# Reciprocals of the attention denominators: from a VectorE reciprocal to a GpSimd power of minus one

## The chip, the cores and the metric

The kernel runs on one core of a Trainium2 chip. The metric is the device time of one execution in microseconds (us). The kernel before has a median of 163.22 us over three runs (163.11, 163.22, 165.66). The engines are written as in the profile: PE (TensorE matmuls), PEld (its weight loads), DVE (VectorE), ACT (ScalarE), POOL (GpSimd), SP (SyncE, whose queue issues all the DMAs here).

## The reference, cut to what matters

Two independent results are put side by side along the last axis: A, a long convolution by FFT over 2048 positions and 576 channels, and B, a block of linear attention with 32 heads of 18 channels. The change touches B alone:

```python
qkv = (x @ wqkv).reshape(B, S, 3, H, Dh)...        # S 2048, D 576, H 32, Dh 18
phi = lambda t: jnp.where(t > 0, t + 1, jnp.exp(t)) + 1e-6
pq, pk = phi(q), phi(k)
kv = jnp.einsum("bhsd,bhse->bhde", pk, v)
z = jnp.einsum("bhsd->bhd", pk)
num = jnp.einsum("bhqd,bhde->bhqe", pq, kv)
den = jnp.einsum("bhqd,bhd->bhq", pq, z)[..., None] + 1e-6
o = num / den
return o... @ wo
```

The division is the place of the change: one denominator for each of 2048 positions and 32 heads, 65536 numbers.

## The kernel before, in words

The kernel is written as a list of operations that are recorded with their reads and writes (`P.op`). The order in which they are issued is fixed by hand-kept text: PLAN (L850 to L887) names the operations one after the other, each with the engine's letter (P, A, D, G for POOL, S for SP) and its number, and PLACES gives each buffer its address. Every engine has its own queue and works it strictly in that order; an instruction that waits holds up all that stand behind it on the same engine. Parts A and B are woven together so that PE has work nearly all the time.

Part A first forms a short convolution of k with four taps and multiplies it with v (`conv_piece`, L384). There are six pieces, three column groups by two halves. Each is two products on DVE (L395, 128x3072), a sum of 3072 and a sum of 1536 (L399 and L402) and a product with v (L404); the sums and the product go through the helper `tt` (L234) on DVE or POOL, as PLAN says. PE then transforms v (`s1`, L456), ACT or DVE copy the result out of PSUM as Cu (L227 and L229 in `copy`), DVE transposes it (L495), PE transforms again (L504), products with the filter's transform follow, and PE transforms back (L540, L565).

Part B projects x to pk (L604, L609, L612) and to pqT (L625, L628, L631), forms G from x and pk (L654), from G the masked matrices kvb (L692) and zsel (L707, L710), and from kvb and wo the matrix M (L751). The denominators follow from pqT and zsel:

- PE forms them in two halves f of 1024 positions (L729). A half lies as 128 partitions x 256 elements: 4 groups of 256 positions by 32 rows for the heads.
- DVE adds a column (L736), which gives `den`, 128x256 float32.
- DVE takes the reciprocal (L742), which gives `rden`, 128x256 bfloat16.
- SP writes `rden` to a scratch in memory (`rw`, twice for each half) and reads it back with each head's row repeated 9 times (`rr`, into `rb`), all L220.
- DVE or POOL multiply pqT by rb (`pqn`, L766, through L234). One of the five pieces of half 0 is on DVE, the other four and all five of half 1 on POOL.
- PE multiplies the normalised pqT by M (L794); the first of these matmuls needs all five pieces of half 0.

The order around the change, from PLAN (L868 to L870):

```
A202 A203 A220 G80 D240 S671 D243 A218
D81 S672 S244 D88 D87 S245 P204 D89 A540 A205 P610 S630 S258 A611 P606 S252 P604 A605 P214 D253 A607 S257 S250 P616
D90 S246 A617 A215 D91 P612 G251 P618
```

D240 and D243 are the two reciprocals. G80 is the sum of 1536 of a convolution piece on POOL, and D81 the product with v that reads G80's result; P610 is the first transform that reads D81's. D88 and D87 are the next piece's two tap products (L395), D89, D90 its sums and D91 its product with v. S244 and S245 write half 0, S258 and S257 half 1, and S252 reads back the piece that D253 multiplies (`pqn` on DVE); S258 stands ahead of S252 on SP. G251 is the first `pqn` on POOL.

Operations marked `two` (the sums and products of two SBUF tensors) have one more rule: when one of them is on POOL, it waits for the last marked operation that DVE has in the order ahead of it (L842 to L847). The reciprocals are not marked.

Of the kernel before, what the change touches and what calls it, by code (L numbers as in the profile page):

```python
# [11 lines left out]
ALU = mybir.AluOpType  # L12

S = 2048
D = 576
EPS = 1e-6
# [97 lines left out]
def _tables():  # L114
    import ml_dtypes
    bf = ml_dtypes.bfloat16
    w0 = 2.0 * np.pi / 8192.0
    k2 = np.arange(128)
    a = np.arange(128)
    b = np.arange(16)  # L120
    n = 16 * a[:, None] + b[None, :]
    ph = ((4 * k2[None, None, :] - 1) * n[:, :, None]) % 8192
    G = np.empty((128, 16, 2, 128), np.float32)
    G[:, :, 0, :] = np.cos(w0 * ph)
    G[:, :, 1, :] = -np.sin(w0 * ph)
    E = np.empty((128, 32 + 2, 128), np.float32)
    phe = ((4 * k2[:, None, None] - 1) * n.T[None, :, :]) % 8192
    E[:, 0:32:2, :] = np.cos(w0 * phe) / 2048.0
    E[:, 1:32:2, :] = -np.sin(w0 * phe) / 2048.0
    W = np.zeros((32, 3, 32), np.float32)  # L130
    for bb in range(16):
        for k1 in range(16):
            p = 2.0 * np.pi * ((k1 * bb) % 16) / 16.0
            c, s = np.cos(p), np.sin(p)
            W[bb, 0, 2 * k1] = c
            W[16 + bb, 0, 2 * k1] = s
            W[bb, 0, 2 * k1 + 1] = -s
            W[16 + bb, 0, 2 * k1 + 1] = c
            W[2 * k1, 1, 2 * bb] = c
            W[2 * k1 + 1, 1, 2 * bb] = -c  # L140
            W[2 * k1, 1, 2 * bb + 1] = s
            W[2 * k1 + 1, 1, 2 * bb + 1] = -s
            W[2 * k1, 2, 2 * bb] = -s
            W[2 * k1 + 1, 2, 2 * bb] = -s
            W[2 * k1, 2, 2 * bb + 1] = c
            W[2 * k1 + 1, 2, 2 * bb + 1] = c
    W[np.abs(W) < 1e-7] = 0.0
    for i in range(2):
        E[:, 32 + i, :] = np.kron(np.eye(4), W[:, 1 + i, :])

    C1 = np.zeros((128, 128 + 32 + 128), np.float32)
    C1[:, 0:128] = np.eye(128)
    C1[:, 128:160] = np.tile(W[:, 0, :], (4, 1))
    C1[:, 160:288] = np.kron(np.eye(4), W[:, 0, :])
    C = np.zeros((128, 32 + 640 + 126 + 8), np.float32)
    o = 0
    hm = np.zeros((128, 5, 128), np.float32)
    for c, (h0, hn) in enumerate(HCH):
        for m in range(hn):
            hm[m, c, 96 + 7 * c + m // 18] = 1.0  # L160
    C[0, o:o + 32] = 1.0
    o += 32
    C[:, o:o + 640] = hm.reshape(128, 640)
    o += 640
    m = np.arange(126)
    C[:126, o:o + 126] = (m[:, None] // 18 == m[None, :] // 18)
    o += 126
    C[:, o:o + 8] = EPS
    return G.astype(bf), E.astype(bf), C1.astype(bf), C.astype(bf)


# [11 lines left out]
def kernel(  # L183
# [13 lines left out]
    nc = tc.nc  # L197
    x, wqkv, wo = B_x[0], B_wqkv, B_wo
    q, k, v = A_q[0], A_k[0], A_v[0]
    outd = out[0]  # L200
    Gt, Et, C1t, Ct = _tables()
    Gp = np.zeros((2, 128, 2304), Gt.dtype)
    Gp[:, :, 0:2048] = Gt.reshape(128, 2, 2048).transpose(1, 0, 2)
# [6 lines left out]
    P = Prog()  # L210
# [25 lines left out]
    def psb(banks, name):  # L236
        return P.buf(name, [128, banks, 512], FP32, space="ps", banks=banks)
# [4 lines left out]
    cst = SB("cst", [128, Ct.shape[1]], side=1)  # L242
# [18 lines left out]
    def cs(o, n):  # L261
        return cst.t[:, o:o + n]
# [28 lines left out]
    for hh in range(2):  # L291
        wps = psb(4, "wps")

        def wmm(e, hh=hh, wps=wps):
# [5 lines left out]
            out=Wj.t[:, :, HALF * hh:HALF * hh + HALF], in_=wps.t[:, :, 0:HALF], func=ACTF.Copy),  # L300
            rd=[wps], wr=[(Wj, hh)], name="Wj", n=1152)
# [367 lines left out]
    for t in range(5):  # L669
# [8 lines left out]
         wr=[(wo5, "m")])  # L678
# [7 lines left out]
    def kvmm(e):  # L686
# [6 lines left out]
        out=kvb.t[0:126, 0:4, :], in0=kps.t[0:126, 0, 0:504].rearrange("p (c m) -> p c m", c=4),  # L693
        in1=maskbd()[0:126, :].unsqueeze(1).to_broadcast([126, 4, 126]), op=ALU.mult),
        rd=[kps, cst], wr=[(kvb, 0)], name="kvev", n=504)
    P.op("D", lambda e: nc.vector.tensor_tensor(
        out=kvb.t[0:72, 4, 0:72], in0=kps.t[0:72, 1, 0:72], in1=maskbd()[0:72, 0:72], op=ALU.mult),
        rd=[kps, cst], wr=[(kvb, 1)], name="kvev", n=72)
    zps = psb(1, "zps")

    def zmm(e):
# [6 lines left out]
        out=zsel.t[0:126, 0:4, :], in0=zps.t[0:126, 0, 0:128].rearrange("p (c m) -> p c m", c=4),  # L708
        in1=hmask()[0:126, 0:4, 96:128], op=ALU.mult), rd=[zps, cst], wr=[(zsel, 0)], name="zev", n=128)
    P.op("D", lambda e: nc.vector.tensor_tensor(  # L710
        out=zsel.t[0:72, 4, :], in0=zps.t[0:72, 0, 128:160], in1=hmask()[0:72, 4, 96:128], op=ALU.mult),
        rd=[zps, cst], wr=[(zsel, 1)], name="zev", n=32)
    dcol = SB("dcol", [128, 1], FP32)
    rdens = []
    for f in range(2):
        dps = psb(2 - f, "dps")
        den = SB("den", [128, 256], FP32)
        rden = SB("rden", [128, 256])
        rdens.append(rden)

        def dmm(e, f=f, dps=dps):
            if f == 0:
                for c, (h0, hn) in enumerate(HCH):
                    for g in range(4):
                        nc.tensor.matmul(dps.t[32 * g:32 * g + 32, 1, 0:1], lhsT=zsel.t[0:hn, c, :], rhs=epsc()[0:hn, :],
                                         start=(c == 0), stop=(c == 4))
            for c, (h0, hn) in enumerate(HCH):
                for g in range(4):
                    nc.tensor.matmul(dps.t[32 * g:32 * g + 32, 0, 0:256], lhsT=zsel.t[0:hn, c, :],  # L729
                                     rhs=pqT[f].t[0:hn, c, 256 * g:256 * g + 256], start=(c == 0), stop=(c == 4))  # L730
        P.op("P", dmm, rd=[zsel] + [(pqT[f], (c, g)) for c in range(5) for g in (2 * f, 2 * f + 1)] + ([cst] if f == 0 else []), wr=[dps],
             name="den", mm=[(256, 128, 128)] * 6)
        if f == 0:
            P.op("D", lambda e, dps=dps: nc.vector.tensor_scalar_add(out=dcol.t[:], in0=dps.t[:, 1, 0:1], scalar1=EPS),
                 rd=[dps], wr=[dcol], name="dcol", n=1)
        P.op("D", lambda e, dps=dps, den=den: nc.vector.tensor_scalar(  # L736
            out=den.t[:], in0=dps.t[:, 0, 0:256], scalar1=dcol.t[:, 0:1], scalar2=None, op0=ALU.add), rd=[dps, dcol],
            wr=[den], name="den+", n=256)

        def rc(e, den=den, rden=rden):  # L740
            with nc.allow_low_precision("as the reference's type"):
                nc.vector.reciprocal(out=rden.t[:], in_=den.t[:])  # L742
        P.op("D", rc, rd=[den], wr=[rden], name="rden", n=256)

    def b_M(c):
        h0, hn = HCH[c]
# [10 lines left out]
    for f in range(2):  # L757
        for i in range(2):
            load("rw", None, lambda e, i=i, f=f: dma(e, ap(r_d, i * S + 1024 * f, [[256, 4], [2 * S, 32], [1, 256]]), rdens[f].t[:]), 65536, 512,
                 rd=[rdens[f]], wr=[(rtok, (f, i))])  # L760
        for c, (h0, hn) in enumerate(HCH):
# [6 lines left out]
                 rd=[rb], wr=[(pqT[f], (c, g)) for g in (2 * f, 2 * f + 1)], name="pqn", n=1024, x2=1, two=1)  # L768
        load("rh", None, lambda e, f=f: dma(e, pqT[f].t[96:128, 4, :], ap(r_d, 1024 * f, [[2 * S, 32], [1, 1024]])), 65536, 2048,
             rd=[(rtok, (f, 0))], wr=[(pqT[f], "r")])  # L770
# [5 lines left out]
    def smm(e):  # L776
# [6 lines left out]
        out=M.t[96:128, 4, :].rearrange("p (h c) -> p h c", h=2), in0=sps.t[96:128, :, 0:HALF], scalar1=EPS, scalar2=None,  # L783
# [152 lines left out]
```

## Time and profile before

| | |
|---|---|
| median of three runs | 163.22 us |
| the profiled execution's own time | 163.43 us |
| its span in the profile | 161.7 us, so 1.73 us lie around it |
| busy share of the span | PE 95%, PEld 74%, DVE 90%, ACT 78%, POOL 35% |
| granted PE clock, mean | 0.997 |
| the two reciprocals (L742, DVE) | 1743 and 1696 ns, 88.92 to 92.27 us |
| the two `den` sums of the same shape (L736, DVE) | 476 and 479 ns |

A line of the engines' order of time gives the start in us from the span's beginning, the duration in us, the engine, the line of the kernel, the operation, output and input with their shapes, and a count where equal neighbours are merged; in brackets stands the time that the engine sat idle before it and what ended that. A DMA on SP (SPq) has the time that SP took to issue it, not that of the transfer. A line of the chain of work that ended last gives start, duration and what the chain passed through; "issue" is time in which the engine waited for nothing that the profile shows, ACTq or DVEq an engine's sequencer. A line of the groups gives the busy time and the mean duration in ns, then the idle time before the group. In the kernel after, every line from L169 on has a number that is one higher.

### The profile page before, as it was taken

The numbers are of one execution on the slowest core, as the hardware profiler recorded it, in microseconds if no ns is written. First come the engines' busy times: TensorE is split into PE (matmuls) and PEld (weight loads), VectorE is DVE, ScalarE is ACT, GpSimd is POOL, SyncE is SP. The second block draws the span as 40 slices with busy tenths as digits, with TensorE's granted clock in tenths as the row PEclk, the third lists the DMA queues.
The fourth block names the chain that finished last, engine by engine and source line by source line (L and its number), as shares of the span: only waits on it lengthen the run. The fifth ranks groups of instructions, "written<-read, shape, count | busy, mean of one in ns | idle before, by whom it ended". The sixth has DMA issues, their size and how long they took to land.

```text
span 161.7 us, 4161 instructions
## 1 busy us (share of the span) xinstructions
PE 153.7 (95%) x1671; PEld 119.6 (74%) x1671; DVE 145.1 (90%) x173; ACT 125.9 (78%) x231; POOL 55.9 (35%) x50
## 2 busy tenths in 40 slices
PE   6899989999999999998999999999999999999991
PEld 2687877644645587896878887887578799999991
DVE  1319999997999999999999999999999999999790
ACT  3139989998988968878645469997999999989512
POOL 8603411110079277051001600999960000002900
PEclk9999999999999999999999999999999999999998
DMA  5999999999930800284940044489996597122975
GB/s 166 288 402 244 232 124 160 309 293 271 401 132 0 292 4 0 41 348 94 334 174 4 18 166 167 158 312 287 299 352 270 155 383 247 65 70 71 264 194 175
DMA packets 25135, 32.20 MB, mean 199 GB/s; under 512 B 15387, under 2 KB 20508, under 8 KB 24348
## 3 DMA queue, kind: packets, MB, share of 16 engines
q1 hardware_dynamic: 25116, 31.94, 65.6%
q8 instruction: 13, 0.21, 0.6%
q14 instruction: 6, 0.05, 0.1%
HBM read 20.27 MB, written 4.98 MB: 156 GB/s over the span
## 4 chain that ended last, share of the span: by engine, by line
PE 57%; DVE 17%; DMA 9%; ACT 5%; SPq 4%; POOL 4%; issue 3%; DVEq 0%; ACTq 0%
PE ps_all L794 13%; PE ps_all L540 10%; PE ps_all L625 10%; PE ps_all L654 6%; PE ps_all L456 6%; PE ps_all L565 5%; DMA hs<-in_A_ssm_k_dram 4%; PE ps_all L504 4%; DVE m L395 4%; DMA kh<-in_A_k_dram 4%; SPq L322 2%; DVE Ch L229 2%; DVE ct L495 2%; DVE rden L742 2%; DVE Cu L229 2%
## 5 line engine op out<-in xcount | busy, mean ns | idle before, releaser
L234 POOL TENSOR_TENSOR m<-m 128x1536 bf16<-128x1536 bf16 x4 | 12.4, 3102 | 34.7 <-DVE m L234 30.7
L625 PE MATMUL ps_all<-xT,wq 128*126 128x512 bf16 (+1 forms) x100 | 24.2, 380 | 0.0
L234 POOL TENSOR_TENSOR pqT<-pqT,rb 126x1024 bf16<-126x1024 bf16 (+1 forms) x9 | 18.9, 2125 | 9.5 <-DVE v L234 9.5
L794 PE MATMUL ps_all<-M,pqT 126*128 126x288 bf16 (+1 forms) x160 | 21.8, 286 | 0.3 <-DVE M L782 0.3
L604 PE MATMUL ps_all<-wk,xT 128*128 128x288 bf16 x160 | 20.7, 286 | 0.6 <-DMA wk<-in_B_wqkv_dram 0.6
L395 DVE TENSOR_TENSOR m<-kh,Wj 128x3072 bf16<-128x3072 bf16 x12 | 20.7, 1767 | 0.3 <-POOL v L234 0.2
L604 PEld LDWEIGHTS <-xT 128*128 128x128 bf16 x160 | 17.3, 110 | 4.0 <-issue 1.5
L456 PEld LDWEIGHTS <-Gsb 128*128 128x128 bf16 x192 | 16.1, 98 | 5.0 <-issue 2.8
L794 PEld LDWEIGHTS <-pqT 126*128 126x128 bf16 (+1 forms) x160 | 16.8, 109 | 3.7 <-issue 1.8
L227 ACT ACTIVATE sph<-ps_all 128x512 bf16<-128x512 f32 x30 | 16.6, 602 | 2.4 <-PE ps_all L504 2.3
L625 PEld LDWEIGHTS <-wq 128*126 128x126 bf16 (+1 forms) x100 | 12.4, 131 | 7.8 <-issue 1.8
L227 ACT ACTIVATE Cu<-ps_all 128x768 bf16<-128x768 f32 x20 | 16.2, 861 | 1.6 <-DVE m L395 0.8
L540 PE MATMUL ps_all<-Esb,sph 128*128 128x128 bf16 x144 | 17.2, 219 | 0.0
L540 PE MATMUL ps_all<-Esb,X 128*128 128x128 bf16 x144 | 17.1, 219 | 0.0
L654 PE MATMUL ps_all<-pk,x_sb 128*128 128x289 bf16 (+1 forms) x128 | 16.8, 287 | 0.0
L227 ACT ACTIVATE V<-ps_all 128x512 bf16<-128x512 f32 x26 | 14.9, 641 | 2.3 <-PE ps_all L540 2.1
L227 ACT ACTIVATE spu<-ps_all 128x512 bf16<-128x512 f32 x28 | 15.4, 619 | 0.6 <-PE ps_all L504 0.6
L609 ACT ACTIVATE ek<-ps_all,neg 128x576 bf16<-128x576 f32 x16 | 11.8, 747 | 4.4 <-PE ps_all L604 3.4
L227 ACT ACTIVATE Ch<-ps_all 128x768 bf16<-128x768 f32 x18 | 14.8, 853 | 0.5 <-PE ps_all L456 0.2
L227 ACT ACTIVATE ob<-ps_all 128x288 bf16<-128x288 f32 x30 | 11.7, 437 | 4.5 <-PE ps_all L794 4.0
L234 POOL TENSOR_TENSOR q<-yb,q 128x768 bf16<-128x768 bf16 x3 | 4.9, 1652 | 28.8 <-PE ps_all L565 28.8
L654 PEld LDWEIGHTS <-x_sb 128*128 128x128 bf16 x128 | 12.4, 98 | 3.0
(94 smaller groups left out, 313.3 us busy)
## 6 DMA issues: line engine op xcount, KB each, us to landing
X<-sph SPq DMA_DIRECT2D x18, 256.0 KB
x_sb<-in_B_x_dram SPq DMA_DIRECT2D x4, 576.0 KB
v<-in_A_v_dram SPq DMA_DIRECT2D x2, 1152.0 KB
out_dram<-ob SPq DMA_DIRECT2D x16, 144.0 KB
q<-in_A_q_dram SPq DMA_DIRECT2D x1, 2304.0 KB
out_dram<-q SPq DMA_DIRECT2D x12, 192.0 KB
rb<-r_scr SPq DMA_DIRECT2D x8, 252.0 KB
kh<-in_A_k_dram SPq DMA_DIRECT2D x1, 1584.0 KB
```

The lines of the kernel that those rows point to most:

```text
L227: nc.scalar.activation(out=o, in_=i, func=ACTF.Copy)
L229: nc.vector.tensor_copy(out=o, in_=i)
L234: return (nc.vector if e == "DVE" else nc.gpsimd).tensor_tensor(out=o, in0=a, in1=b, op=op)
L395: return nc.vector.tensor_tensor(out=m.t[:, i:i + 2], in0=i0, in1=i1, op=ALU.mult)
L456: nc.tensor.matmul(ps.t[:, bank, lo - 384 * bank:hi - 384 * bank], lhsT=Gsb.t[:, b, ri, :], rhs=src[:, lo - CC * j:hi - CC * j], start=Tru ...
L540: nc.tensor.matmul(ps.t[:, 0, 128 * c:128 * c + 128], lhsT=src.t[:, 4 * hh + c, :], rhs=Esb.t[:, 32 + wi, :], start=(wi == 0), stop=(wi == 1))
L565: nc.tensor.matmul(ps.t[:, 0, n * j:n * j + n], lhsT=Esb.t[:, 2 * b + ri, :], rhs=V[gi].t[:, 2 * b + ri, :], start=(ri == 0), stop=(ri == 1))
L604: nc.tensor.matmul(ps.t[:, hh, 0:HALF], lhsT=cols(xT.t[0:KT[t], t, :], r), rhs=wk.t[0:KT[t], t, HALF * hh:HALF * hh + HALF], start=(t == 0 ...
L609: P.op("A", lambda e: nc.scalar.activation(out=eb.t[:], in_=ps.t[:, :, 0:HALF], func=ACTF.Exp, bias=neg1.t[:]), rd=[ps, neg1], wr=[eb], na ...
L625: nc.tensor.matmul(ps.t[0:hn, 0, :], lhsT=wq.t[0:KT[t], t, h0:h0 + hn], rhs=xT.t[0:KT[t], t, :], start=(t == 0), stop=(t == 4))
L654: nc.tensor.matmul(ps.t[0:m, 0, 0:n], lhsT=x4[r // 4].t[:, r % 4, :] if t == 4 else x_sb[r // 4].t[:, r % 4, 128 * t:128 * t + 128], rhs=p ...
L794: nc.tensor.matmul(ps.t[:, 0, 0:HALF], lhsT=cols(pqT[r // 8].t[0:kn, c, 512 * (r // 4 % 2):512 * (r // 4 % 2) + 512], r), rhs=M.t[0:kn, c, ...
```

## The change

The two reciprocals are computed on POOL as `den` to the power of minus one, by a product-like instruction of two tensors. The exponent is read from a constant table in SBUF: of the eight constant columns that held 1e-6, four now hold -1.0, and one of these, a bfloat16 column of 128x1, is repeated over the 256 elements. The operation reads the constants as well (`cst`). The PLAN and PLACES texts are the same, so PLAN's letter for the two operations is still D, and the instruction is issued to POOL's queue at the same place in the order: on POOL behind G80 and ahead of G251, and gone from DVE between the `den` sums and D81. The operations' marks are the same: the power is not marked `two`.

```diff
-    C[:, o:o + 8] = EPS
+    C[:, o:o + 4] = EPS
+    C[:, o + 4:o + 8] = -1.0
...
         def rc(e, den=den, rden=rden):
             with nc.allow_low_precision("as the reference's type"):
-                nc.vector.reciprocal(out=rden.t[:], in_=den.t[:])
-        P.op("D", rc, rd=[den], wr=[rden], name="rden", n=256)
+                nc.gpsimd.tensor_tensor(out=rden.t[:], in0=den.t[:], in1=cs(802, 1).to_broadcast([128, 256]), op=ALU.pow)
+        P.op("D", rc, rd=[den, cst], wr=[rden], name="rden", n=256)
```

## The prediction

> **What bounds the kernel now.** I read the engines' totals first, then the stages, then the chain of work that ended last around the reciprocals, and then the queues that meet there.
>
> ```profile
> PE 153.7 (95%) x1671; PEld 119.6 (74%) x1671; DVE 145.1 (90%) x173; ACT 125.9 (78%) x231; POOL 55.9 (35%) x50
> ...
> 90.00:100.00 10.00, 9.86 (x89) 8.09 (x88) 9.90 (x9) 6.54 (x13) 1.46 (x1) 1.00 0.39 132
> 100.00:110.00 10.00, 9.55 (x121) 7.92 (x119) 9.88 (x12) 9.39 (x15) 9.06 (x5) 1.00 0.67 227
> 110.00:130.00 20.00, 19.73 (x272) 14.77 (x260) 19.83 (x23) 19.58 (x48) 9.82 (x5) 1.00 0.81 273
> ```
>
> The first line is the page's, the others are stages (length, then busy us of PE, PEld, DVE, ACT, POOL). Between 90 and 130 us PE is idle for 0.14 + 0.45 + 0.27 = 0.86 us only. Freeing DVE can save no more than that before PE itself is the bound. DVE is nearly as full (9.90 of 10), so both queues have almost no slack in which a delay could vanish.
>
> The chain runs straight through the reciprocals:
>
> ```profile
> 88.14 0.87 DVE den L736 x2
> 89.01 3.27 DVE rden L742 x2
> 92.28 0.82 DVE v L234
> 93.10 0.02 issue
> 93.13 3.44 DVE m L395 x2
> 96.56 0.03 ACTq L227
> ...
> 96.64 2.34 ACT Cu L227 x3
> ...
> 99.02 0.49 PE ps_all L456 x4
> ```
>
> To be seen: 3.27 us of chain belong to the change, and behind them the product v, the tap products m, ACT's copies and PE follow within 0.1 us of each other. What delays v delays PE.
>
> POOL's and SP's queues in order of time:
>
> ```profile
> 88.36 3.09 POOL L234 TENSOR_TENSOR m<-m 128x1536 bf16<-128x1536 bf16 x1 [14.91 <-DVE m L234]
> 100.94 18.93 POOL L234 TENSOR_TENSOR pqT<-pqT,rb 126x1024 bf16<-126x1024 bf16 x9 [9.48 <-DVE v L234]
> ```
>
> ```profile
> 90.69 1.24 SPq L220 DMA_DIRECT2D r_scr<-rden  x2
> 92.03 0.52 SPq L220 DMA_DIRECT2D X<-sph  x1
> 92.64 0.52 SPq L220 DMA_DIRECT2D r_scr<-rden  x1
> 94.01 0.88 SPq L220 DMA_DIRECT2D rb<-r_scr  x1
> ```
>
> POOL looks free from 91.45 to 100.94, but it is busy with G80 from 88.36 to 91.45, just when `den` is ready (89.01).
>
> **What goes.** Two reciprocals, 1743 + 1696 ns with overlap 3.35 us of DVE. But the next DVE instruction, v, reads what POOL's sum G80 writes, and that ends at 88.36 + 3.09 = 91.45. In the chain v starts at 92.28; without the reciprocals it could start at about 91.50. The removal is worth 0.78 us, not 3.35; for the other 2.5 us DVE would stand idle behind POOL.
>
> **What comes.** Two powers of 128x256 on POOL, the first at about 91.50 (queue order: G80 is ahead), which is 2.5 us later than the reciprocal started. Call one power p. The trace has no power on POOL, so p is bounded. Lower end: a plain POOL two-tensor operation. The rows 128x1536 (3102 ns) and 128x768 (1652 ns) give (3102 - 1652)/768 = 1.89 ns an element and 0.20 us fixed, so 0.20 + 256 x 1.89 ns = 0.69 us. One step up: on DVE the reciprocal costs 1720/478 = 3.6 times the plain operation of the same shape; with this factor on POOL's element part, 0.20 + 3.6 x 0.48 = 1.9 us. A power with a free exponent is more than a reciprocal: it is the exponential of a product with a logarithm, each a series of multiplications and additions with splitting and joining of the exponent around it. If each of these steps costs one plain pass of 0.48 us, 11 steps give 5.5 us and 30 steps 14.7 us. The counts are my estimate, the price of a step is the row's. I take p = 5.5 us, nearest to the row of plain operations that still counts both functions as short series; the ends kept are 0.69 and 14.7.
>
> **Who shares with whom.** From 91.5 on DVE has seven operations in a row that read two SBUF tensors (v, two tap products, sum, pqT, sum, v). The trace shows what POOL and such an operation do to each other:
>
> ```profile
> 5.48 0.40 POOL L231 COPY x<-x_sb 128x256 bf16<-128x256 bf16 x1
> ...
> 51.51 1.93 POOL L231 COPY x<-x_sb 128x256 bf16<-128x256 bf16 x1
> ```
>
> ```profile
> 51.43 1.75 DVE L395 TENSOR_TENSOR m<-kh,Wj 128x3072 bf16<-128x3072 bf16 x1
> ...
> 53.10 1.94 DVE L395 TENSOR_TENSOR m<-kh,Wj 128x3072 bf16<-128x3072 bf16 x1
> ```
>
> The same POOL copy takes 0.40 us alone and 1.93 us when it starts 0.08 us behind a tap product; it ends at 53.44, 0.26 us after that product's end at 53.18, and the second tap product ends 0.2 us late. They took turns, whole instruction by whole instruction. The Trainium skill, "SBUF — State Buffer", section "SBUF: two separate sides", states this as a rule: GpSimd and a DVE operation with two SBUF inputs share a port pair by an exclusive lock, held for the full instruction. The copy agrees with it; no run yet shows it for an operation that computes long.
>
> So I let the two powers and DVE's products take turns: both powers and v are done at 91.50 + 2p + 0.82, and everything behind v on DVE is late by 2p - 0.78. With p = 5.5: 10.2 us.
>
> **The memory round trip.** rden of half 0 is there at 91.5 + p = 97.0, of half 1 at 91.5 + 2p = 102.5 (with v between the powers, 103.3), against 90.7 and 92.3. On SP the write S258 of half 1 stands ahead of S252, the read that DVE's pqT needs, so this read waits for the second power too: issued about 0.6 us behind it, near 103.9. Before, it was issued at 94.01 and DVE went into pqT at 98.26 without a wait, so it takes at most 4.25 us; by the 0.88 us of issue and the 2 us from the writes' issue (91.9) to the read that waits for them (94.0), about 3. It lands at 106.9 to 108.2, and DVE reaches pqT at 98.26 + 10.2 = 108.5. The round trip is just hidden; without the lock it would be the limit. The X transfer queued behind the first writes, and the other reads, move by the same amount with their users.
>
> **What hides nothing.** POOL's nine pqn pieces wait for DVE's v (100.81) and move with it; the four of half 0 end at 109.33, 1.2 us ahead of the first L794. PE waits for v's result at 95.1 and for ACT's Cu at 99.0. PE is full from there to the end and cannot catch up. The constants' table has the same size: nothing, as PE reads the table at 82.2 us already (L703).
>
> **Sum.** The span of 161.7 becomes 161.7 - 0.78 + 2 x 5.5 = 171.9; with the 1.73 us around it 173.6. The profiled run (163.43) stands 0.2 us above the median.
>
> The Trainium skill, "TensorE: Matmul & The Clock Gate", Part 1, says that PE's clock halves after an idle window of about 3.4 us and comes back after as long a busy one. Here the granted clock is 1.00 in all stages from 0 to 150 us and PE's longest wait is 1.5 us, so this trace cannot show it; by the page each long wait would add up to 1.7 us, and one of them would make the sum 175.3.
>
> **The rivals.**
> *The power is cheap, no change.* It decides from 2p - 0.78 = 3.26 us, p = 2.0 us, that is 3.8 plain passes. For it: the DVE factor of 3.6 gives 1.9 us. Against: the free exponent. At p = 0.69 the time is 163.43 + 0.6 = 164.0, at p = 1.9 it is 166.5. The most that could be gained, with the powers hidden altogether, is 0.78 us: 162.7. A gain of 2% (3.27 us) has no room, as PE has 0.86 us of idle time from 90 to 130.
> *The power runs in many more steps.* At 20 steps p = 9.9 and the time is 182.4; at 30, p = 14.7 and 192.0. For it: no row shows a cheap function on POOL. Against: nothing but the guess of short series.
> *The lock does not hold while the power computes.* Then DVE runs v and the taps beside it and gets to pqT at 97.5, where it waits for the read: issued at 102.5 + 0.6, landed 106.1 to 107.4, so 7.8 to 9.1 us late instead of 10.2, 171.3 to 172.5. What speaks for it: a power needs its port for a small part of its time. Against: the 1.93 us copy.
> *DVE wins the port each time.* Then the first power starts only when DVE stops at pqT (97.5), and the delay is 2p + 2.9 = 13.9: 177.3. Against: the copy got in between two tap products.
>
> **How the numbers follow.** p from 2.0 to about 9: 0.55 with the taking of turns as the likeliest way (the two variants of the port lie 1 to 4 us around it); p below 2.0: 0.15; more steps than 18: 0.30. The predicted time is 173.6; alone its case runs from 167 to 181. The range for 8 in 10 goes down to the plain price, 164.0, and up to 30 steps, 192.0; left out are 0.05 below and 0.15 above. Chances: faster by over 2% 0.02 (only if a part of the reasoning on PE fails), within 2% 0.13, slower by over 2% 0.85. Two per cent is about what a measurement of this kernel can tell from no change.
>
> **What would show it.** Right: two POOL groups at the power's line from 91.5 on, each of several us; DVE idle from 89.0 to 91.5 and again, or with lengthened v and tap products, beside the powers; ACT's Cu, PE's L456 and the first L794 late by the same amount; all else of unchanged duration. DVE's products at their old 0.9 and 1.7 us beside a running power would refute the lock, a granted clock below 1 around 100 us would speak for the clock rule, and a power under 2 us would leave nothing of the forecast but the 0.78 us. The forecast is wrong in size if p is, for the delay goes with twice p.

## The result, and the profile after

The kernel after takes 243.98 us (median of 4 runs, 243.91 to 244.39) against 163.29 us before: a ratio of 1.495 with a 95% interval of 1.492 to 1.498. It is far slower, by 80.7 us. The forecast was 173.6 us in a range of 164.0 to 192.0: the sign is right, but the change is nearly eight times the 10.4 us that were forecast.

The totals and four stages of the profile after (length, then busy us of PE, PEld, DVE, ACT and POOL with instructions in brackets, granted PE clock, DMA share, GB/s):

```profile
PE 154.7 (64%) x1671; PEld 120.5 (50%) x1671; DVE 142.4 (59%) x171; ACT 126.0 (52%) x231; POOL 138.0 (57%) x52
```

```profile
80.00:91.00 11.00, 11.00 (x148) 8.96 (x146) 9.05 (x11) 5.70 (x11) 2.52 (x1) 1.00 0.28 86
91.00:130.00 39.00, 10.30 (x92) 8.31 (x90) 6.54 (x4) 8.15 (x14) 39.00 (x2) 0.68 0.00 0
130.00:160.00 30.00, 0.00 (x0) 0.00 (x0) 0.00 (x0) 0.00 (x0) 30.00 (x2) 0.50 0.04 13
160.00:175.00 15.00, 0.00 (x0) 0.00 (x0) 0.00 (x0) 0.00 (x0) 13.76 (x1) 0.50 0.00 0
```

PE's busy time is 1.0 us above before, DVE's 2.7 below; only POOL's has grown, by 82.1. Between 130 and 173 us no engine but POOL computes anything. The chain of work that ended last says the same (start, duration, what it passed through):

```profile
91.53 82.24 POOL rden L743 x2
...
173.78 0.51 SPq L221
...
174.47 3.33 DMA rb<-r_scr
...
177.82 0.69 DVE pqT L235
...
180.43 2.10 PE ps_all L457 x12
```

Where 3.27 us of reciprocals stood, 82.24 us of powers stand. They start at 91.53, where the forecast put them. One power takes this long:

```profile
L743 POOL TENSOR_TENSOR rden<-den,cst x2: 41127/41132/41137, 91.5 to 132.6; 128x256 bf16<-128x256 f32 x2
```

Minimum, median and maximum are within 10 ns, so neither a first use nor a neighbour is in it. DVE beside them, in order of time:

```profile
91.60 1.35 DVE L235 TENSOR_TENSOR v<-m,v 128x1536 bf16<-128x1536 bf16 x1 [2.48 <-POOL m L235]
92.98 3.43 DVE L396 TENSOR_TENSOR m<-kh,Wj 128x3072 bf16<-128x3072 bf16 x2
96.45 1.76 DVE L235 TENSOR_TENSOR m<-m 128x3072 bf16<-128x3072 bf16 x1
177.82 0.69 DVE L235 TENSOR_TENSOR pqT<-pqT,rb 126x1024 bf16<-126x1024 bf16 x1 [79.61 <-DMA rb<-r_scr]
```

The product v is 0.45 us longer than before (0.90); the tap products and the sum have their old lengths although the power runs beside them. Then DVE waits 79.61 us for rb, the read-back of the reciprocals. So DVE was not held by taking turns with POOL, but by the round trip through memory. SP's queue shows why this waits for both powers:

```profile
132.69 1.23 SPq L221 DMA_DIRECT2D r_scr<-rden  x2
134.02 0.52 SPq L221 DMA_DIRECT2D X<-sph  x1
173.78 0.51 SPq L221 DMA_DIRECT2D r_scr<-rden  x1
174.47 0.88 SPq L221 DMA_DIRECT2D rb<-r_scr  x1
```

Half 0 is written at 132.69, but the read of it stands behind the first write of half 1, which waits for the second power until 173.77.

### The profile page after: what moved, and what is told of

It reads as the page before. It is cut to its first block, busy times and chain, and to the rows that moved or that the text cites. A ratio compares the mean times of both kernels' runs of the same rounds, so it can differ in the third digit from the quotient of the medians.

```text
span 242.1 us, 4163 instructions
## 1 busy us (share of the span) xinstructions
PE 154.7 (64%) x1671; PEld 120.5 (50%) x1671; DVE 142.4 (59%) x171; ACT 126.0 (52%) x231; POOL 138.0 (57%) x52
## 4 chain that ended last, share of the span: by engine, by line
PE 39%; POOL 38%; DVE 8%; DMA 7%; ACT 2%; issue 2%; SPq 1%; POOLq 0%; DVEq 0%; ACTq 0%
POOL rden L743 34%; PE ps_all L795 8%; PE ps_all L541 7%; PE ps_all L626 6%; PE ps_all L457 4%; PE ps_all L566 3%; PE ps_all L655 3%; PE ps_all L505 3%; DMA wk<-in_B_wqkv_dram 3%; DMA kh<-in_A_k_dram 2%; POOL pqT L235 2%; PE ps_all L605 2%; DVE Ch L230 1%; DVE m L396 1%; POOL m L235 1%
## 5 line engine op out<-in xcount | busy, mean ns | idle before, releaser
L743 POOL TENSOR_TENSOR rden<-den,cst 128x256 bf16<-128x256 f32 x2 | 82.2, 41132 | 0.0
L457 PE MATMUL ps_all<-v,Gsb 128*128 128x192 bf16 x96 | 11.2, 261 | 79.3 <-DVE v L235 79.1
L457 PEld LDWEIGHTS <-Gsb 128*128 128x128 bf16 x192 | 16.7, 101 | 84.1 <-DVE v L235 79.4
L235 DVE TENSOR_TENSOR pqT<-pqT,rb 126x1024 bf16<-126x1024 bf16 x1 | 0.7, 692 | 79.6 <-DMA rb<-r_scr 79.6
## 6 DMA issues: line engine op xcount, KB each, us to landing
out_dram<-q SPq DMA_DIRECT2D x12, 192.0 KB
```

The lines of the kernel that those rows point to most:

```text
L235: return (nc.vector if e == "DVE" else nc.gpsimd).tensor_tensor(out=o, in0=a, in1=b, op=op)
L457: nc.tensor.matmul(ps.t[:, bank, lo - 384 * bank:hi - 384 * bank], lhsT=Gsb.t[:, b, ri, :], rhs=src[:, lo - CC * j:hi - CC * j], start=Tru ...
L743: nc.gpsimd.tensor_tensor(out=rden.t[:], in0=den.t[:], in1=cs(802, 1).to_broadcast([128, 256]), op=ALU.pow)
```

## The experiments

**What costs 41 us: the function or its operands.** The multiplication leaves the inversion out: den is negated.

```diff
-                nc.gpsimd.tensor_tensor(out=rden.t[:], in0=den.t[:], in1=cs(802, 1).to_broadcast([128, 256]), op=ALU.pow)
+                nc.gpsimd.tensor_tensor(out=rden.t[:], in0=den.t[:], in1=cs(802, 1).to_broadcast([128, 256]), op=ALU.mult)
```

> The kernel after with a multiplication in place of the power: same engine, same queue place, same operands (float32 den, a bfloat16 column repeated, bfloat16 out). The output is not the reference's, as den is negated and not inverted. Theory F (the function is what costs 41 us): about 0.7 us for each operation, and the whole within 1 us of the kernel before, 163 to 164 us. Rival O (the float32 operand, the mixed types or the repeated column are slow on POOL): each operation stays at tens of us and the time near 244. In the trace, if POOL and a DVE product of two SBUF tensors take turns, DVE's v (0.9 us) starting beside the first multiplication is lengthened by about its remaining length, to 1.3 to 1.6 us; if they do not, it stays at 0.9.

Measured: 163.79 us, ratio 1.0042 (1.0027 to 1.0056). The two multiplications took 614 and 1330 ns:

```profile
L743 POOL TENSOR_TENSOR rden<-den,cst x2: 614/972/1330, 91.2 to 91.7; 128x256 bf16<-128x256 f32 x2
```

```profile
91.23 1.35 DVE L235 TENSOR_TENSOR v<-m,v 128x1536 bf16<-128x1536 bf16 x1 [2.48 <-POOL m L235]
92.62 3.72 DVE L396 TENSOR_TENSOR m<-kh,Wj 128x3072 bf16<-128x3072 bf16 x2
96.37 1.76 DVE L235 TENSOR_TENSOR m<-m 128x3072 bf16<-128x3072 bf16 x1
98.29 0.69 DVE L235 TENSOR_TENSOR pqT<-pqT,rb 126x1024 bf16<-126x1024 bf16 x1 [0.16 <-DMA rb<-r_scr]
```

Theory F holds: engine, place, float32 input and repeated column cost 0.6 us; the power costs 40.5 more. Here the taking of turns is seen: v waits for the first multiplication, the second (1330 ns) for v, and a tap product for the second. The move to POOL with a cheap function is no gain either: the time is 0.4% longer, which is within 2%.

**What the function's cost depends on.** Single operations behind the end of the kernel before, one to a line of the kernel (L860 to L867); L868 is a reciprocal on DVE. The inputs `sin` and `di` are filled with 3.0; `ex(n)` repeats a column of -1.0 over n elements, and column 16 of `sx` holds 2.0.

```diff
...
+            nc.gpsimd.tensor_tensor(out=so[:], in0=sin[:], in1=ex(256), op=ALU.pow)
+            nc.gpsimd.tensor_tensor(out=so[:, 0:128], in0=sin[:, 0:128], in1=ex(128), op=ALU.pow)
+            nc.gpsimd.tensor_tensor(out=so[:, 0:64], in0=sin[:, 0:64], in1=ex(64), op=ALU.pow)
+            nc.gpsimd.tensor_tensor(out=so[0:8, :], in0=sin[0:8, :], in1=ex(256, 8), op=ALU.pow)
+            nc.gpsimd.tensor_tensor(out=so[:, 0:128], in0=sin[:, 0:128], in1=sin[:, 128:256], op=ALU.pow)
+            nc.gpsimd.tensor_tensor(out=so[:, 0:128], in0=sin[:, 0:128], in1=sx[:, 16:17].to_broadcast([128, 128]), op=ALU.pow)
+            nc.gpsimd.tensor_tensor(out=so[0:64, :], in0=sin[0:64, :], in1=ex(256, 64), op=ALU.pow)
+            nc.gpsimd.tensor_tensor(out=so[:], in0=sin[:], in1=ex(256), op=ALU.mult)
+            nc.vector.reciprocal(out=do[:], in_=di[:])
```

> The kernel before, and behind its end a row of single operations on a scratch of threes, whose result nobody uses: on POOL the power with exponent -1 on 128x256, 128x128, 128x64, 8x256 and 64x256, a power of two full float32 tensors 128x128, exponent 2 on 128x128, and a multiplication 128x256; on DVE one reciprocal. Theory F1 (a routine run for each element of a partition, 16 partitions at a time): 160 ns an element, so 41, 20.6 and 10.3 us for 256, 128 and 64; 41 us for 64 and for 8 partitions alike; 20.6 us for the full tensors and for exponent 2. Rival F2 (a large fixed cost for each instruction): the three sizes differ by far less than their ratio. Rival F3 (each lane by itself in turn): 8 partitions cost about half. Rival F4 (repeated multiplication for whole exponents): exponent 2 costs a small part. The time of the whole is about 163 plus 41 + 20.6 + 10.3 + 41 + 20.6 + 20.6 + 41 = 358 us by F1.

Measured, in one execution: 361.56 us in all, and in POOL's order of time:

```profile
161.77 41.14 POOL L860 TENSOR_TENSOR bench_out<-bench_in,bench_x 128x256 bf16<-128x256 f32 x1
202.99 20.72 POOL L861 TENSOR_TENSOR bench_out<-bench_in,bench_x 128x128 bf16<-128x128 f32 x1
223.79 10.52 POOL L862 TENSOR_TENSOR bench_out<-bench_in,bench_x 128x64 bf16<-128x64 f32 x1
234.39 41.11 POOL L863 TENSOR_TENSOR bench_out<-bench_in,bench_x 8x256 bf16<-8x256 f32 x1
275.57 20.78 POOL L864 TENSOR_TENSOR bench_out<-bench_in 128x128 bf16<-128x128 f32 x1
296.43 20.72 POOL L865 TENSOR_TENSOR bench_out<-bench_in,bench_x 128x128 bf16<-128x128 f32 x1
317.22 41.11 POOL L866 TENSOR_TENSOR bench_out<-bench_in,bench_x 64x256 bf16<-64x256 f32 x1
358.41 0.61 POOL L867 TENSOR_TENSOR bench_out<-bench_in,bench_x 128x256 bf16<-128x256 f32 x1
```

From 64 to 256 elements the time grows by (41.14 - 10.52)/192 = 159.5 ns an element, with 0.3 us fixed. 8, 64 and 128 partitions cost the same, and so do exponent -1, exponent 2 and a full tensor of exponents. So the proportion that F1 gives holds, and F2, F3 and F4 fall. That a routine runs, and 16 partitions at a time, is not shown: whatever works through the elements of a partition one by one, with the partitions side by side, would take these times. The multiplication beside them takes 0.61 us, DVE's reciprocal of the same shape 1753 ns: the power is 67 times the one and 23 times the other. Other values than 3.0 and other input types than float32 were not tried here; the denominators themselves cost the same 41.13.

**Whether the queues or the data carry the delay.** Only half 1 goes to POOL.

```diff
-        def rc(e, den=den, rden=rden):
+        def rc(e, den=den, rden=rden, f=f):
...
+                if f == 0:
+                    return nc.vector.reciprocal(out=rden.t[:], in_=den.t[:])
                 nc.gpsimd.tensor_tensor(out=rden.t[:], in0=den.t[:], in1=cs(802, 1).to_broadcast([128, 256]), op=ALU.pow)
```

> Half 0 is inverted on DVE as before, only half 1 by the power on POOL. Theory Q (what stands behind the power in the queues waits for it, whatever half it needs): SP's write of half 1 stands ahead of the read-back that DVE's pqT of half 0 needs, so pqT starts near 136.7 us of the span instead of 98.3, and the time is 163.4 + 38.5 and about 0.9 for the slower PE clock, 202.8 us. Rival N (only the data of half 1 is late): DVE's pqT starts near 98.3, and the next limit is POOL's own queue, whose pqn pieces of half 0 stand behind the power: first L794 at 141 instead of 110.5, time about 194 to 195.

Measured: 202.67 us, ratio 1.241 (1.239 to 1.244). SP and DVE in order of time:

```profile
90.83 1.23 SPq L221 DMA_DIRECT2D r_scr<-rden  x2
92.16 0.52 SPq L221 DMA_DIRECT2D X<-sph  x1
132.73 0.51 SPq L221 DMA_DIRECT2D r_scr<-rden  x1
133.35 0.89 SPq L221 DMA_DIRECT2D rb<-r_scr  x1
```

```profile
136.47 0.69 DVE L235 TENSOR_TENSOR pqT<-pqT,rb 126x1024 bf16<-126x1024 bf16 x1 [38.23 <-DMA rb<-r_scr]
```

Half 0 is written to memory at 90.83, yet DVE gets it at 136.47: Theory Q, within 0.3 us of its number. No number that pqT reads was late; its load stood behind a write that waited. In this order POOL's pieces of half 0 stand behind the power as well, so putting the load ahead on SP alone would not have saved it; a new order of both queues was not tried.

**What removing the reciprocals is worth.** Left out of the kernel before altogether: the sum on DVE that gave `den` now writes `rden` itself, so pqT is multiplied by the denominators.

```diff
...
-                nc.vector.reciprocal(out=rden.t[:], in_=den.t[:])
-        P.op("D", rc, rd=[den], wr=[rden], name="rden", n=256)
...
+            nc.vector.tensor_scalar(
+                out=rden.t[:], in0=dps.t[:, 0, 0:256], scalar1=dcol.t[:, 0:1], scalar2=None, op0=ALU.add)
+        P.op("D", rc, rd=[dps, dcol, den], wr=[rden], name="rden", n=256)
```

> The reciprocals are left out of the kernel before: the den sum on DVE writes rden itself, so pqT is multiplied by the denominator instead of its inverse, and nothing is added on POOL. Theory G (v behind them waits for POOL's sum until 91.5 us, so the removal frees 0.8 us of the chain): 162.4 to 162.8 us, DVE idle about 2.5 us ahead of v. Rival R (the whole 3.35 us comes out of the chain): 160.0 to 160.4 us.

Measured: 162.84 us against 163.25 us of the kernel before beside it, ratio 0.9985 (0.9959 to 1.0011); the span of the profiled run is 161.0 against 161.7.

```profile
91.33 0.96 DVE L234 TENSOR_TENSOR v<-m,v 128x1536 bf16<-128x1536 bf16 x1 [1.40 <-POOL m L234]
92.32 3.43 DVE L395 TENSOR_TENSOR m<-kh,Wj 128x3072 bf16<-128x3072 bf16 x2
```

The product v still waits for POOL's sum. Rival R (3 us) is excluded. The medians differ by 0.41 us, half of the 0.78 of Theory G, and the interval does not tell this from none. Of the 0.7 us between the two spans, 0.16 stand already ahead of the change: POOL's sum starts at 88.20 here and at 88.36 in the profile before. So, in this order, no other engine for these reciprocals could have brought more than some tenths of a us.

**The rest: PE's clock after the wait.** In the kernel with half 1 on POOL, PE gets something to do while it waits. The base was run again beside it.

```diff
+                    if nm == "u" and cc == 2 and (ri, bg) == (0, 2):
+                        for _ in range(170):
+                            nc.tensor.matmul(ps.t[:, 0, :], lhsT=Gsb.t[:, 0, 0, :],
+                                             rhs=Gsb.t[:, 1:3].rearrange("p a b c -> p (a b c)"), start=True, stop=True)
```

> The kernel with half 1 alone inverted by the power on POOL once more, as the base for the next: 202.6 to 202.8 us.

> The same kernel with 170 idle matmuls of 128x512 put ahead of the transform L456 on which PE waits 37.7 us for DVE's v; their result is overwritten. At 216 ns each they fill about 36.7 us of the wait. Theory C (about 0.9 us of the loss is PE's halved clock after the wait): the granted clock stays at 1.0 and the time falls to about 201.8 us. Rival W (the rest of the loss is transfers and queues after the wait): unchanged, 202.6 to 202.8.

Measured: 203.19 us without and 201.30 us with the idle matmuls. The same stages of the one and of the other (columns as above):

```profile
100.00:138.00 38.00, 1.26 (x11) 0.77 (x8) 1.61 (x3) 1.80 (x3) 32.62 (x1) 0.55 0.06 19
138.00:145.00 7.00, 6.03 (x49) 5.82 (x50) 5.32 (x7) 3.12 (x5) 5.95 (x3) 0.53 0.48 169
```

```profile
100.00:138.00 38.00, 37.51 (x175) 17.27 (x177) 1.79 (x3) 1.57 (x3) 32.40 (x1) 1.00 0.06 20
138.00:145.00 7.00, 5.38 (x63) 4.66 (x63) 6.91 (x9) 5.37 (x8) 6.14 (x3) 1.00 0.66 233
```

With work in the wait the clock stays at 1.00, and the kernel with 170 more matmuls is 1.9 us faster: Theory C, at twice the size expected. How far the slow clock reaches behind the wait is not the same in every run. In this profile without idle matmuls PE starts again at 138.97 and the clock is 0.50 until 144 and 1.00 from 145 us; in the earlier run of the same kernel (half 1 on POOL, 202.67 us) PE starts at 139.08, and the clock is 0.50 until 142 and 1.00 from 143. What it costs can be read from the piece of `M` that DVE writes and PE's matmuls with pqT need, without and with the idle matmuls:

```profile
149.58 0.76 DVE L785 TENSOR_SCALAR M<-ps_all 32x576 bf16<-32x576 f32 x1
```

```profile
147.64 0.76 DVE L789 TENSOR_SCALAR M<-ps_all 32x576 bf16<-32x576 f32 x1
```

From the start of pqT (136.36 and 136.18) these are 13.22 and 11.46 us; 11.46 is also the distance in the kernel before. In the earlier run it is 12.37. So one wait cost 0.9 us in one profile and 1.8 in the other. The base without idle matmuls varies by 0.5 us between the two times that it was run (202.67 and 203.19), and whether that is the clock too is not shown.

**Whether the power shares an access with DVE.** Two stages behind the end of the kernel before: 20 DVE products of two SBUF tensors (L868) beside one power (L866), then 12 (L875) and a DVE copy (L870) beside three plain POOL products (L871 to L873).

```diff
+            nc.gpsimd.tensor_tensor(out=so[:], in0=pin[:], in1=sx[:, 0:1].to_broadcast([128, 256]), op=ALU.pow)
+            for _ in range(20):
+                nc.vector.tensor_tensor(out=db[:], in0=da[:], in1=db[:], op=ALU.mult)
...
+            nc.vector.tensor_copy(out=gd[:], in_=go[:])
+            nc.gpsimd.tensor_tensor(out=pa[:], in0=pa[:], in1=pa[:], op=ALU.mult)
...
+            for _ in range(12):
+                nc.vector.tensor_tensor(out=db[:], in0=da[:], in1=db[:], op=ALU.mult)
```

> The kernel before, and behind its end two stages on scratch whose result nobody uses. Stage 1: one power of 128x256 on POOL, and beside it 20 products of two SBUF tensors 128x1536 on DVE, each 0.9 to 1.0 us alone. Stage 2: three products of 128x1536 on POOL, 3.1 us each alone, and beside them 12 such products on DVE. Theory A (the power holds the shared access for a moment at its start, a plain POOL product for its whole length): in stage 1 the first DVE product takes about 1.4 us and the others 0.9 to 1.0, and the power 41.1; in stage 2 the engines take turns, one DVE product after each POOL product is lengthened by up to 3 us, or the POOL products are. Rival L (the lock holds for the whole instruction, and DVE's products beside the power in the kernel after ran in some gap of it): in stage 1 a DVE product is lengthened by tens of us or the power by the products. Rival S (no lock at all, a shared bandwidth): in stage 2 all products are lengthened a little and alike.

Measured, in one execution, by line (minimum, median and maximum in ns), with two lines of the order of time:

```profile
L866 POOL TENSOR_TENSOR bench_out<-bench_in,bench_x x1: 41175/41175/41175, 162.2 to 162.2; 128x256 bf16<-128x256 f32 x1
```

```profile
L868 DVE TENSOR_TENSOR bench_db<-bench_da,bench_db x20: 957/959/1377, 162.3 to 181.6; 128x1536 bf16<-128x1536 bf16 x20
```

```profile
162.20 0.17 DVE L865 COPY bench_gd<-bench_go 128x16 bf16<-128x16 bf16 x1 [0.30 <-POOL bench_go L864]
```

```profile
203.39 2.75 POOL L871 TENSOR_TENSOR bench_pa<-bench_pa 128x1536 bf16<-128x1536 bf16 x1
```

```profile
L870 DVE COPY bench_gd<-bench_go x1: 2692/2692/2692, 203.5 to 203.5; 128x16 bf16<-128x16 bf16 x1
```

```profile
L875 DVE TENSOR_TENSOR bench_db<-bench_da,bench_db x12: 945/959/3384, 206.1 to 221.8; 128x1536 bf16<-128x1536 bf16 x12
```

Theory A: beside the power one DVE product of the twenty is 0.42 us longer and the median is unmoved at 0.96; the power loses 0.04 us. Beside plain POOL products a DVE copy that took 0.17 us in stage 1 takes 2.69, until the POOL product ends, and two products of 0.96 us take 3.38. So both halves are seen with the same instruments: the plain product excludes DVE for its whole length, the power for about 0.4 us near its start. Just where these 0.4 us lie is not shown, as the copy of stage 1 starts 0.01 us behind the power and is not held. The multiplication held v as long as the power did (1.35 us in both kernels). Rivals L and S fall.

## Why the prediction was right or wrong

**The step that failed** is the price of one power, "11 steps give 5.5 us and 30 steps 14.7 us". It measured 41.13 us: 7.5 times the value taken and 2.8 times the upper end. In passes of 0.48 us it is 85 instead of 11. The price of a pass was the row of a plain operation on two tensors, but no row showed that a power is made of such passes, or of how many. Nothing in the trace bounded it from above, so the "upper end" was a guess dressed in a row's unit, and the range inherited it. With p twice in the sum, the error of 35.6 us became 71. What the 41.13 us are spent on stays open: the runs show only that they go with the number of elements in a partition and come with the power and not with its operands.

**The form of the sum was nearly right, by a rival's path.** With p = 41.13 the forecast's 161.7 - 0.78 + 2p gives a span of 243.2; the profile has 242.1. But it is right for a wrong reason: the turns ("both powers and v are done at 91.50 + 2p + 0.82") did not happen, and v ended at 92.95. The path is that of the third rival, where the read-back is the limit: second power done 173.77, read issued 174.47, landed 177.80, DVE 79.56 us later than before (177.82 against 98.26). With p = 41.13 that rival's own terms have the read land at 177.4 to 178.6. The remaining 80.4 - 79.56 = 0.84 us of span comes behind that, with PE at half clock: DVE's kvb reads PE's kv product, which is done at 184.39 only, and M follows. Before, and after:

```profile
104.14 0.19 DVE L696 TENSOR_TENSOR kvb<-ps_all,cst 72x72 bf16<-72x72 f32 x1
109.72 0.76 DVE L782 TENSOR_SCALAR M<-ps_all 32x576 bf16<-32x576 f32 x1
```

```profile
184.58 0.23 DVE L697 TENSOR_TENSOR kvb<-ps_all,cst 72x72 bf16<-72x72 f32 x1 [0.81 <-issue]
190.20 0.77 DVE L783 TENSOR_SCALAR M<-ps_all 32x576 bf16<-32x576 f32 x1
```

They start 80.44 and 80.48 us later.

**The memory round trip** was read correctly: S258 ahead of S252 on SP makes half 0 wait for half 1's power. It was forecast as just hidden, and it is what ended last; the experiment with one half shows it alone.

**What goes** was right about the wait: v waits for POOL's sum (91.6 after), and the trial without reciprocals gains 0.4 us by the medians, not 3.35; the 0.78 of the forecast was not reached. One reading beside it was wrong without touching the number: PE does not wait for v at 95.1 us. In the profile before, v is done at 93.10, and PE has other matmuls without a gap from 89.19 to 95.10.

**The lock** failed as the forecast put it. The Trainium skill, "SBUF — State Buffer", section "SBUF: two separate sides", has the pair held for the full instruction. By that, the powers would have lengthened DVE's products by tens of us. The plain products agree with the page (2.69 us for a copy of 0.17), the power does not (0.4 us of 41). The measurement decides: the rule does not hold for this power, which takes 41.13 us where a multiplication of the same operands takes 0.61.

**The clock** was right in kind and left out of the sum. The Trainium skill, "TensorE: Matmul & The Clock Gate", Part 1, has the clock at half after an idle window: the traces agree in kind, with 0.50 in the waits and 1.00 where PE had matmuls. In time they spread: the clock fell 2 to 4 us after PE's last matmul (at 101.3 us, with the fall between 105.0 and 105.5 in the kernel after and between 103.5 and 104.0 with half 1 alone) and came back 3 to 6 us after the first one. In the kernel after, PE's twelve L457 matmuls took 2.10 us instead of 1.15 and the 25 of the kv product 2.07 instead of 1.48, and the price is the 0.84 us above; in the experiment with idle matmuls it was 1.9. The estimate that the prediction drew from that page, up to 1.7 us for a long wait, lies between the two.

**The chances.** Slower by over 2% had 0.85 and came true; the case of more steps had 0.30, of which 0.15 lay above the range, and no case held the value itself.

## What to carry to other kernels

A function that no row of the trace shows has no upper bound from rows of other functions: run it once behind the end of a kernel before moving it, or leave the range open above. An engine's idle share says nothing about a move to it: 35% busy POOL had room for two cheap operations, not for 82 us, and what was taken away on DVE was mostly covered by another wait. Look at what stands behind the moved step's readers in each queue: here one late write held a read of other data, and with it the whole core.

## What the runs showed of the hardware

- GpSimd's power costs 159.5 ns for each element of a partition and 0.3 us fixed, for 8 to 128 partitions and for the exponents -1, 2 and 3 alike; the multiplication of the same shape 0.61 us.
- A plain GpSimd product of two tensors excluded a DVE operation for its whole 2.75 us; a power of 41.17 us for about 0.4 us only.
- The granted PE clock fell to 0.50 within 2 to 4 us of a wait of 38 or 79 us and stayed there for 3 to 6 us of work behind it (0.53 from 138 to 145 us in one run); matmuls without use in the wait kept it at 1.00, and the time was 1.9 us shorter.
